# An attention-plus-MLP kernel on one core: the hand order of head pairs 0 to 17 written anew, banks taken by a ring, two halves of the norms issued apart, 67 zero products instead of 116

## The chip, the cores and the metric

The kernel runs on one core of a Trainium2 chip. A core has a matrix engine (PE, with its weight loads shown apart as PEld), a vector engine (DVE), a scalar engine (ACT), a general engine (POOL) and a queue engine (SP), each with its own instruction stream that is worked off in order, and DMA queues. The engines meet through semaphores. The metric is the device time of one execution in microseconds. A profiled execution gives the span and the trace; the times come from other executions, which carry no profile.

## The reference: what is computed

Cosine attention over 8 batches of 12 heads, 448 positions and 64 channels, then an MLP with a hard-swish between its two products:

```python
q_n = q / (np.linalg.norm(q, axis=-1, keepdims=True) + 1e-06)
k_n = k / (np.linalg.norm(k, axis=-1, keepdims=True) + 1e-06)
scores = np.matmul(q_n, k_n.transpose(0, 1, 3, 2)) / tau
...
attn = np.exp(scores)
attn = attn / (np.sum(attn, axis=-1, keepdims=True) + 1e-09)
return np.matmul(attn, v).astype(np.float32)
...
h = x @ w_in                          # x: 3584 x 768, w_in: 768 x 2048
relu6 = np.clip(h + 3.0, 0.0, 6.0)
g = h * relu6 / 6.0
return (g @ w_out).astype(np.float32) # w_out: 2048 x 768
```

Inputs and output are float32; tau is 0.1.

## The kernel before

The 96 heads are worked as 48 pairs, six pairs to a batch. The 448 positions of a head lie as 64 rows of 7 slots. An item `j` is the queries or the keys of two pairs, four heads (item 0 the queries and item 1 the keys of pairs 0 and 1, items 2 and 3 those of pairs 2 and 3, and so on; from item 14 on the order of queries and keys is turned round). An item is loaded, squared, reduced to its sums of squares, given its inverse norms, multiplied by them into bf16, and transposed. Items 0 to 13 are transposed on PE into a PSUM bank and copied out of it; from item 14 on a transposing DMA does it.

For each pair the scores come in four groups (three of two 128-key tiles, one for the last 64 keys of both heads), each is turned into exponentials by ACT, and PE multiplies the exponentials with the values and a column of ones, so that the row sums come along. DVE divides, and the result is transposed to be the input `xT` of the MLP of its batch: PE works six products for each 128 of the 2048 hidden channels (L591), ACT makes `u` (L608), DVE makes `gT` (L614). The second MLP product is taken as seven products over two by two blocks with sums of blocks formed beforehand on DVE (`w_sum` at L697, `gs` at L726, products at L751).

Nothing is scheduled by a planner at run time: the order on every engine is the order in which the Python code issues the instructions. For pairs 18 to 47 a loop issues them; for pairs 0 to 17, the start included, the order is written out by hand in `PLAN`, a list of strings whose words are operations. The words that the prediction uses, with the function and the line of each:

- `LQ.j`, `LV.d`: SP issues the load of an item (L201) and the four loads of the values of two pairs (L216). A buffer is loaded again only when its last reader is done.
- `SQ.j.e.c.n`: squares n of an item's slots from slot c on engine e (v for DVE, a for ACT, p for POOL; L231 or L233).
- `RE.j`: DVE adds the squares (L245).
- `NO.d`: the inverse norms of both items of d, first two small ACT instructions (L275, L276), then two on DVE where the word ends in v (L278, L279), two more on ACT where not. `NO.d.x` is one item. `NN.8` does two at once.
- `NM.j.e`: the item times its inverse norms (L292). With `.0` or `.1` behind it, one half.
- `TR.j`: seven transposes on PE into a bank (L338), which Y or Z behind it names. `XD.j`: the transposing DMA issued by SP (L349) with its two small POOL copies.
- `CQ.i`, `CK.i`, `CS.i`: queries and keys of pair i copied out of the bank or the transposed tile to where PE reads them (L358 ACT, L360 DVE, L388 DVE from the DMA's tile).
- `SC.i.g`, `EX.i.g`, `VA.i.g`, `FI.i`: scores (L441), exponentials (L459), values (L481) and the division (L501, L502).
- `BK.i`, `CX.i`: the transposes of the result on PE (L515) and the copy to `xT`; `XP`, `XB` do it by DMA.
- `VC.i`: the values of a pair cast to bf16 (L309, L311).
- `W`: POOL issues a load of weights (L921). `WS`, `GS`: sums of weight or activation blocks (L697, L726).
- `UH.n.k`, `U`: parts of the first MLP product, whole units of either product; `UA` and `UV` issue the ACT and DVE work that such a unit leaves (`u`, `gT`).
- `DP.n`: n zero products into a corner of the bank PV that nobody reads (L933). `D.1`: one into Y.

PSUM has eight banks. Two are PV. Until `OPEN` (after the exponentials of pair 5) four serve as two wide score buffers `SC0` and `SC1`; Y and Z are named by the words for transposes. From `OPEN` on, the four and Y and Z form a ring of six, out of which each result takes the next bank, while some words still name Y or Z:

```python
bank = {"Y": Y, "Z": Z}[name] if name else next_bank()
```

A bank is written again when its last reader is done; that wait stands on PE.

Of the kernel before, what the change touches and what calls it, by code (L numbers as in the profile page):

```python
# [66 lines left out]
def kernel(
# [857 lines left out]
    def busy(n):  # L925
        bank_of("Y", 0)
        for _ in range(n):
            nc.tensor.matmul(Y[:, :], zeros[:, 0:128], zeros[:, :], start=True, stop=True)
# [182 lines left out]
```

## Time and profile before

| what | before |
|---|---|
| median of 3 executions | 401.87 us (401.65 to 402.15) |
| the profiled execution's span | 403.6 us |
| PE busy, matmuls | 394.2 us, 98% |
| DVE busy | 297.2 us, 74% |
| ACT busy | 277.4 us, 69% |
| POOL busy | 233.1 us, 58% |
| zero products | 116 into PV, 18.3 us of PE's busy time |

The span of the profiled execution is 1.7 us above the median of those without a profile. Busy shares are means over the whole span; the front, where the items of the first pairs are prepared, differs from the rest, so the prediction reads the profile by stretches. In a timeline row the first number is the start in us, the second the time in which the row's instructions ran, then engine, line, operation, the tile written and read, the shapes and the count; brackets hold the idle time ahead of it and what ended it. Instructions of one engine overlap by some tenths of a microsecond, so a row's time is a little more than the distance to the next start.

### The profile page before, as it was taken

Reading aid. Unit: us, or ns where it says so; the run is one execution under the profiler, and the core shown is the slowest. Engines: PE = TensorE matmul, PEld = TensorE weight load, DVE = VectorE, ACT = ScalarE, POOL = GpSimd, SP = SyncE. Lnnn points to the kernel's source line nnn. Section 1 sums busy time; section 2 is a strip of 40 time slices with the busy share of each in tenths; the row PEclk is TensorE's granted clock in tenths of the full one; section 3 lists DMA queues with packets and bytes.
Section 4 is the critical chain, followed back from the end, with each engine's and each line's share of the span. In section 5 each row is a group of like instructions: output and inputs, shape, how many; then the busy total and the mean of one; then the engine's idle time right before and its main releaser. Section 6 shows DMA issues by size and latency. Waiting matters only on the chain.

```text
span 403.6 us, 9692 instructions
## 1 busy us (share of the span) xinstructions
PE 394.2 (98%) x3708; PEld 234.7 (58%) x3709; DVE 297.2 (74%) x535; ACT 277.4 (69%) x602; POOL 233.1 (58%) x234
## 2 busy tenths in 40 slices
PE   8999999989999999999999999999999999999996
PEld 7666556545565556555555556555565556555563
DVE  7898898899868777767867887587656566654663
ACT  5799889886677686786858768668758755225230
POOL 6799709660675896479385876866665500510070
PEclk9999999999999999999999999999999999999999
DMA  8989989998679469696899647866883523130134
GB/s 288 291 209 231 222 179 278 168 231 203 173 149 242 97 149 198 170 200 135 174 209 206 151 118 167 179 184 137 192 154 72 112 45 66 42 79 21 24 74 98
DMA packets 93166, 63.75 MB, mean 158 GB/s; under 512 B 56128, under 2 KB 93120, under 8 KB 93120
## 3 DMA queue, kind: packets, MB, share of 16 engines
q1 hardware_dynamic: 87408, 56.45, 60.9%
q0 software_dynamic: 5312, 6.29, 9.3%
q8 instruction: 29, 0.48, 0.5%
q10 hardware_dynamic: 400, 0.39, 0.3%
q14 instruction: 17, 0.14, 0.1%
HBM read 45.61 MB, written 11.01 MB: 140 GB/s over the span
## 4 chain that ended last, share of the span: by engine, by line
PE 80%; DVE 5%; POOL 4%; DMA 3%; issue 3%; ACT 3%; SPq 0%; POOLq 0%; DVEq 0%
PE M L591 21%; PE M L751 17%; PE PV L481 10%; PE Y L751 6%; PE M L441 5%; PE Z L751 5%; PE Z L591 4%; PE Y L591 3%; PE M L831 3%; ACT at L459 2%; DMA big<-in_k_dram 2%; POOL nrm L292 2%; POOL big L233 2%; DMA tT<-nrm 2%; PE Z L831 1%
## 5 line engine op out<-in xcount | busy, mean ns | idle before, releaser
L591 PE MATMUL M<-xT,w_in_sb 128*128 128x448 bf16 x540 | 114.6, 352 | 0.2 <-DVE gT L614 0.2
L459 ACT ACTIVATE at<-M 128x448 bf16<-128x448 f32 x195 | 96.7, 566 | 20.0 <-PE M L441 10.1
L591 PEld LDWEIGHTS <-w_in_sb 128*128 128x128 bf16 x768 | 72.3, 98 | 64.2 <-issue 3.8
L233 POOL TENSOR_TENSOR big<-big 128x896 f32<-128x896 f32 (+5 forms) x47 | 69.5, 1481 | 23.0 <-DMA big<-in_k_dram 10.4
L292 POOL TENSOR_TENSOR nrm<-big,r 128x896 bf16<-128x896 f32 (+1 forms) x45 | 74.6, 1660 | 10.2 <-ACT r L282 5.5
L614 DVE SCALAR_TENSOR_TENSOR gT<-u,M 128x448 bf16<-128x448 bf16 x80 | 48.9, 617 | 35.2 <-ACT u L608 34.7
L608 ACT ACTIVATE u<-M,bias 128x448 bf16<-128x448 f32 x90 | 58.1, 651 | 22.9 <-PE M L591 22.2
L481 PEld LDWEIGHTS <-at 128*128 128x128 bf16 (+1 forms) x1536 | 53.8, 97 | 20.4 <-issue 10.6
L481 PE MATMUL PV<-vx,at 128*128 128x65 bf16 (+1 forms) x1536 | 62.2, 193 | 0.1
L245 DVE TENSOR_REDUCE n<-big 128x14 f32<-128x896 f32 (+1 forms) x50 | 51.6, 1038 | 2.1 <-POOL big L233 1.9
L398 POOL COPY km<-tT 64x128 bf16<-64x128 bf16 x34 | 12.7, 373 | 59.1 <-PE M L441 25.1
L780 POOL TENSOR_TENSOR big<-big 128x384 f32<-128x384 f32 x12 | 12.4, 1036 | 59.4 <-ACT big L799 59.4
L751 PEld LDWEIGHTS <-gT 128*128 128x128 bf16 x320 | 30.8, 98 | 22.0 <-DVE gT L726 0.8
L502 DVE TENSOR_TENSOR on<-PV,rc 128x512 bf16<-128x512 f32 x48 | 33.2, 691 | 1.7
L441 PE MATMUL M<-tT,kz 64*128 64x448 bf16 (+1 forms) x175 | 31.7, 351 | 1.7 <-DVE gT L614 1.4
L751 PEld LDWEIGHTS <-gs 128*128 128x128 bf16 x248 | 23.7, 98 | 16.3 <-DVE gs L726 0.8
L459 ACT ACTIVATE at<-Y 128x448 bf16<-128x448 f32 x51 | 28.8, 565 | 6.1 <-PE Z L441 6.0
L751 PE MATMUL M<-w_out_sb,gT 128*128 128x384 bf16 x176 | 32.2, 326 | 0.3 <-DVE gT L726 0.3
L459 ACT ACTIVATE at<-Z 128x448 bf16<-128x448 f32 x48 | 27.0, 562 | 3.8 <-PE M L441 1.9
L751 PE MATMUL M<-w_sum,gs 128*128 128x384 bf16 (+1 forms) x168 | 29.1, 318 | 0.0
L726 DVE TENSOR_TENSOR gs<-gT 128x1024 bf16<-128x1024 bf16 x30 | 28.9, 962 | 0.0
L591 PE MATMUL Z<-xT,w_in_sb 128*128 128x448 bf16 x132 | 28.6, 352 | 0.0
(131 smaller groups left out, 569.7 us busy)
## 6 DMA issues: line engine op xcount, KB each, us to landing
big<-in_k_dram SPq DMA_DIRECT2D x24, 448.0 KB, 4.6
big<-in_q_dram SPq DMA_DIRECT2D x24, 448.0 KB, 4.7
out_dram<-o SPq DMA_DIRECT2D x107, 96.0 KB, 2.2
big<-in_v_dram SPq DMA_DIRECT2D x48, 128.0 KB, 4.2
big<-in_v_dram SPq DMA_DIRECT2D x48, 96.0 KB, 4.2
w_in_sb<-in_moe_w_in_dram POOLq DMA_DIRECT2D x8, 384.0 KB, 7.8
w_out_sb<-in_moe_w_out_dram POOLq DMA_DIRECT2D x4, 768.0 KB, 11.7
tT<-nrm SPq DMA_TRANSPOSE x34, 3.0
```

Of the source, the lines that this page charges most:

```text
L233: engines[e].tensor_tensor(out=o, in0=i, in1=i, op=ALU.mult)
L245: nc.vector.tensor_reduce(out=n2_and_r[0][:, d % 2, j % 2, c], in_=sq[:, :, :, :].rearrange("p g c d -> p (g c) d")[:, c, :], axis=AX.X, o ...
L292: engines[e].tensor_tensor(out=nrm[:, :, g, :].rearrange("p c g d -> p g c d"), in0=raw_of[j][:, g, :, :], in1=n2_and_r[2][:, d % 2, j % 2, :]
L441: nc.tensor.matmul(o, ks, qt[rows], start=True, stop=True)
L459: nc.scalar.activation(out=o, in_=x, func=AF.Exp, scale=inv_tau)
L481: nc.tensor.matmul(pv_out(j, h), at[rows, n, q_cols(i // HP, j)], vt[rows, 3 + h if name == "M" else 5 * h + int(name[1]), :], start=(name ...
L502: nc.vector.tensor_tensor(out=on[:, :, :, :].rearrange("p j h d -> p h j d"), in0=pv4[:, :, :, 0:D], in1=rc[:, :, :].to_broadcast([128, 2, ...
L591: nc.tensor.matmul(ps[:, 0:S], w_in_sb[:, cc, fc * 128 : (fc + 1) * 128], xT[b % 2][:, cc, 0:S], start=(cc == 0), stop=(cc == CC - 1), ski ...
L608: nc.scalar.activation(out=u[:, :], in_=ps[:, 0:S], func=AF.Relu, bias=half_bias, scale=1.0 / 6.0)
L614: nc.vector.scalar_tensor_tensor(out=g[:, fc, c0 : c0 + S], in0=u[:, :], scalar=1.0, in1=ps[:, 0:S], op0=ALU.min, op1=ALU.mult,)
L726: nc.vector.tensor_tensor(out=o[:, :, :], in0=x, in1=y, op=op)
L751: nc.tensor.matmul(m, lhs[:, c, :], rhs[:, c, c0 : c0 + width], start=(base is None and c == 0), stop=(c == KC - 1), skip_group_check=True,)
```

## The change

`PLAN` is replaced by another order of almost the same words. The words in which the two differ: 67 zero products (`DP`) instead of 116 and no `D.1`; `NO.d` split into `NA.d` (the two ACT instructions) and `NV.d` (the rest) for d of 0 to 7 and 10; `CK.3` on ACT instead of DVE, `CK.18` on DVE instead of ACT; `VC.12` on ACT instead of POOL, `VC.13` on POOL instead of ACT, `VC.18` on DVE instead of POOL, `VC.19` on ACT instead of DVE; `NM.20` on POOL instead of DVE. No transposes name their bank any more: each result's bank is given by one digit of `RING`, and behind its end the ring of six goes on.

```diff
 PLAN = [
-    "LQ.1 SQ.1.v.0.4 DP.3 DP.5 DP.1 DP.1 DP.1 DP.1 DP.2 DP.1 DP.2 DP.6 DP.2 DP.2 DP.1 DP.1 DP.2 DP.1 DP.1 DP.1",
-    "SQ.1.a.11.3 SQ.1.p.4.3 DP.1 DP.2 DP.3 SQ.1.a.7.4 RE.1.0 DP.1 DP.4 LQ.0 DP.2 SQ.0.p.0.6 DP.1 RE.1.1 DP.1 LQ.3",
-    "DP.1 SQ.3.p.0.4 DP.1 SQ.0.a.6.2 SQ.0.a.8.6 DP.1 DP.1 RE.0.0 DP.1 RE.0.1 LQ.2 NO.0.1 NM.1.v.0 NM.1.v.1 SQ.3.a.4.3",
-    "NO.0.0 NM.0.p.1 DP.2 DP.2 SQ.2.a.4.3 TR.1.Z NM.0.p.0 LQ.5 SQ.2.a.0.4 D.1 DP.1 RE.3 DP.1 CK.0.a SQ.5.p.0.4 DP.2",
-    "SQ.5.a.4.3 DP.2 RE.2 NO.1.v DP.3 DP.2 DP.1 TR.0.Y LQ.4 CQ.0.a SQ.4.p.4.3 DP.2 SQ.4.a.0.4 DP.3 NM.3.p DP.1 RE.5",
-    "CQ.1.v RE.4 LV.0 SC.0.0.0 LQ.6 DP.3 VC.0.v NM.2.v.1 EX.0.0 SC.0.1.1 NM.2.p.0 CK.1.v LQ.7 LQ.8 DP.5 EX.0.1",
-    "SC.0.2.0 EX.0.2 DP.1 VC.1.v DP.1 DP.1 SC.0.3.1 EX.0.3 DP.2 VA.0.0 DP.2 LV.1 SQ.6.p.0.7 VA.0.1 SC.1.0.0 NO.2.v",
-    "NM.4.v.1 SC.1.1.1 TR.2.Y DP.1 NM.4.p.0 SQ.7.a.4.3 DP.1 RE.6 DP.1 DP.1 EX.1.0 EX.1.1 SC.1.2.0 TR.3.Z EX.1.2",
-    "CK.2.v DP.1 CQ.2.v SQ.7.p.0.4 DP.1 DP.1 VA.0.2 VA.0.3 SQ.8.a.4.3 NM.5.p SC.1.3.1 VC.3.p LQ.10 FI.0 EX.1.3 LQ.9",
...
+    "LQ.1 SQ.1.p.4.3 LQ.0 SQ.1.a.11.3 SQ.0.p.0.6 SQ.1.a.7.4 SQ.1.v.0.4 RE.1.1 SQ.0.a.8.6 SQ.0.a.6.2 LQ.3 RE.1.0",
+    "NA.0.1 NV.0.1 SQ.3.a.4.3 SQ.3.p.0.4 LQ.2 RE.0.1 RE.0.0 NM.1.v.0 NA.0.0 NV.0.0 SQ.2.a.4.3 NM.0.p.0 NM.1.v.1 LQ.6",
+    "LQ.5 SQ.2.a.0.4 DP.6 DP.6 DP.6 DP.6 DP.6 DP.6 DP.6 DP.2 TR.1 CK.0.a RE.3 RE.2 NM.0.p.1 SQ.5.p.0.4 DP.6 DP.2 TR.0",
+    "CQ.1.v NA.1 SQ.5.a.4.3 NV.1.v CQ.0.a LQ.4 DP.6 DP.2 SC.0.0.0 SQ.4.p.4.3 CK.1.v SQ.4.a.0.4 RE.5 LV.0 NM.2.p.0",
+    "VC.0.v RE.4 NM.2.v.1 SC.0.1.1 EX.0.0 DP.5 SC.0.2.0 EX.0.1 LV.1 VA.0.0 SC.0.3.1 EX.0.2 DP.2 SC.1.0.0 NM.3.p",
+    "SQ.6.p.0.7 VC.1.v LQ.7 EX.0.3 LQ.8 SC.1.1.1 NA.2 EX.1.0 NV.2.v NM.4.v.1 VA.0.1 NM.4.p.0 TR.2 SQ.7.p.0.4 SC.1.2.0",
+    "SQ.7.a.4.3 EX.1.1 LQ.9 EX.1.2 VA.0.2 TR.3 RE.6 SC.1.3.1 LQ.10 VA.0.3 CK.2.v CQ.2.v SQ.8.a.4.3 FI.0 LQ.11",
+    "SC.2.0.0 EX.1.3 SC.2.1.1 NM.5.p LV.2 SQ.8.a.0.4 RE.7 RE.8 LV.3 EX.2.0 CK.3.a VA.1.0 VC.2.v VA.1.1 EX.2.1 VC.3.p",
...
```

The words around the stretch of 60 to 90 us, before and after:

```diff
-    "EX.11.3 UA TR.12 CQ.13.v SQ.16.p.6.1 UV CQ.12.a SQ.17.p.0.7 CS.13.v NO.7.v U VA.11.1 VA.11.2 NM.14.p UA UV LQ.19",
-    "SC.12.0 EX.12.0 VA.11.3.t FI.11 SC.12.1 RE.16 LQ.18 U LV.6 EX.12.1 VC.12.p UA LV.7 UV SC.12.2 BK.9 NM.15.p",
-    "SQ.18.p.4.3 U SQ.18.a.0.4 CX.9.v U RE.17 UA BK.8.Z VA.12.0 UV CX.8.v EX.12.2 UA BK.10 SC.12.3 EX.12.3 CX.10.v",
-    "VA.12.1 VC.14.p SQ.19.p.0.7 XD.15 BK.11 CX.11.a U UA UV RE.18 XD.14 SC.13.0 SC.13.1 EX.13.0 W W LQ.21 U VA.12.2",
-    "UV VA.12.3.t RE.19 SC.13.2 UA UV U EX.13.1 SC.13.3 VC.13.a UA NN.8 WS.1.0 NM.16.p WS.7.0 CK.15.v EX.13.2",
-    "SQ.21.p.4.3 CK.14.a U U NM.18.p WS.6.0 EX.13.3 CS.14.v FI.12 XD.16 U U UV SC.14.0 UA UA UV UV U VA.13.0",
...
+    "SQ.16.p.6.1 CQ.12.a U VA.11.1 UV NV.7.v UA VA.11.2 NM.14.p SC.12.0 EX.12.0 LV.7 VA.11.3.t LQ.18 SC.12.1 U UV",
+    "FI.11 EX.12.1 RE.16 VC.14.p UA SC.12.2 UV LV.6 VC.12.a BK.9 U CX.9.v SQ.18.p.4.3 U BK.8 SQ.18.a.0.4 NM.15.p",
+    "XD.14 UA UV VA.12.0 RE.17 EX.12.2 BK.10 CX.8.v SC.12.3 VA.12.1 UA XD.15 CX.10.v LQ.21 BK.11 EX.12.3 CX.11.a U",
+    "SC.13.0 UV SQ.19.p.0.7 UA RE.18 EX.13.0 U VA.12.2 UV RE.19 VA.12.3.t SC.13.1 SC.13.2 UA EX.13.1 UV U UA W NN.8 W",
+    "CK.14.a VC.13.p WS.7.0 EX.13.2 SC.13.3 NM.16.p CK.15.v EX.13.3 U U U SQ.21.p.4.3 WS.1.0 NM.18.p WS.6.0 U FI.12",
+    "UV UA UV SC.14.0 UA UV VA.13.0 U U SQ.21.a.0.4 CS.14.v RE.21 UA VA.13.1 LQ.23 UV GS.6 VA.13.2 EX.14.0 VC.15.a",
...
```

(From pair 14 on `CK` is a DVE copy whatever letter stands behind it.) The code beside it:

```diff
+RING = "233223223323450123450123450123450123450123450123450123450123450123450123450123450123450123501234501234501234501234501234501234501234501234501234"
...
-    ring = []
+    ring = [None, None, Y, Z, None, None]
     ring_n = [0]
 
     def next_bank():
+        n = ring_n[0]
         ring_n[0] += 1
-        return ring[(ring_n[0] - 1) % len(ring)]
+        return ring[int(RING[n]) if n < len(RING) else (n - len(RING) + int(RING[-1]) + 1) % len(ring)]
...
+    def norms_root(d, *items):
         needs(("NM", 2 * d - 4), ("NM", 2 * d - 3))
-        items = items or (0, 1)
+        items, tiles, pairs = norm_tiles(d, items)
         for x in items:
             needs(("RE", 2 * d + x))
...
+        root(tiles, pairs)
+
+    def norms_inverse(d, *args):
+        items, tiles, pairs = norm_tiles(d, args)
+        inverse(tiles, pairs, "v" in args)
         for x in items:
             issued.add(("NO", d, x))
...
+    def root(tiles, pairs):
         n2, le, r = tiles
         ln, nr = n2, pairs[:, :, :, 0]
         nc.scalar.activation(out=ln, in_=n2, func=AF.Ln)
         nc.scalar.activation(out=nr, in_=ln, func=AF.Exp, scale=0.5)
+
+    def inverse(tiles, pairs, on_vector):
...
-        bank = {"Y": Y, "Z": Z}[name] if name else next_bank()
+        bank = next_bank()
```

The loop for pairs 18 to 47, the MLP products and the loads' sizes are as before.

More of the change, by code (lines that the diff above doesn't have):

```diff
@@ L251, in reduce, with norm_tiles @@
         whole("RE", j, heads)
+    def norm_tiles(d, items):
+        items = tuple(x for x in items if x != "v") or (0, 1)
+        it = slice(items[0], items[-1] + 1)
+        return items, [t[:, d % 2, it, :] for t in n2_and_r], nr_eps[:, d % 2, it, :, :]
     def norms(d, *items):
-        on_vector, items = "v" in items, tuple(x for x in items if x != "v")
+        norms_root(d, *items)
+        norms_inverse(d, *items)
+    def norms_root(d, *items):
         needs(("NM", 2 * d - 4), ("NM", 2 * d - 3))
-        items = items or (0, 1)
+        items, tiles, pairs = norm_tiles(d, items)
         for x in items:
             needs(("RE", 2 * d + x))
-        it = slice(items[0], items[-1] + 1)
-        inverse([t[:, d % 2, it, :] for t in n2_and_r], nr_eps[:, d % 2, it, :, :], on_vector)
+        root(tiles, pairs)
+    def norms_inverse(d, *args):
+        items, tiles, pairs = norm_tiles(d, args)
+        inverse(tiles, pairs, "v" in args)
         for x in items:
@@ L268, in norms_two @@
         two = [t.rearrange("p e i c -> p (e i) c") for t in n2_and_r]
-        inverse(two, nr_eps.rearrange("p e i c x -> p (e i) c x"), on_vector)
+        pairs = nr_eps.rearrange("p e i c x -> p (e i) c x")
+        root(two, pairs)
+        inverse(two, pairs, on_vector)
         issued.update(("NO", x, y) for x in (d, d + 1) for y in range(2))
-    def inverse(tiles, pairs, on_vector):
+    def root(tiles, pairs):
         n2, le, r = tiles
@@ L276, in inverse @@
         nc.scalar.activation(out=nr, in_=ln, func=AF.Exp, scale=0.5)
+    def inverse(tiles, pairs, on_vector):
+        n2, le, r = tiles
+        nr = pairs[:, :, :, 0]
         if on_vector:
@@ L921, in next_weights @@
         nc.gpsimd.dma_start(out=o, in_=w)
[L925 to L928, printed above, removed]
     def busy_pv(n):
@@ L941, in open_ring @@
         m = [psum_m.tile([128, 512], FP32, name=f"M{n}", tag=f"M{n}") for n in range(4)]
-        ring.extend([m[0], m[1], Y, Z, m[2], m[3]])
+        ring[:] = [m[0], m[1], Y, Z, m[2], m[3]]
     def unit():
@@ L958 @@
     OPS = {
-        "LQ": load_qk, "LV": load_v, "W": next_weights, "SQ": square, "RE": reduce, "NO": norms, "NN": norms_two,
+        "LQ": load_qk, "LV": load_v, "W": next_weights, "SQ": square, "RE": reduce, "NO": norms, "NA": norms_root, "NV": norms_inverse, "NN": norms_two,
         "NM": normalise, "VC": vcast, "TR": transposes, "XD": crossbar, "XB": back_crossbar, "XP": back_two, "CQ": copy_q, "CK": copy_k, "CS": copy_k3, "SC": scores,
         "EX": exps, "VA": values, "FI": finish_values, "BK": back, "CX": copy_x, "U": unit, "UH": lambda n, k, bank=None: mm1_piece(0, n, CUTS[k], CUTS[k + 1], bank), "UA": lambda: finish_units("a"), "UV": lambda: finish_units("v"), "UP": lambda: finish_units("p"), "GS": lambda x, *n: g_sum(*((0, "e") if x == "e" else (-1, str(x)))),
-        "GL": g_left, "WS": lambda x, *h: weight_sums(str(x), *((h[0] * KC // 2, KC // 2) if h else (0, KC))), "UU": whole_units, "D": busy, "DP": busy_pv, "OPEN": open_ring,
+        "GL": g_left, "WS": lambda x, *h: weight_sums(str(x), *((h[0] * KC // 2, KC // 2) if h else (0, KC))), "UU": whole_units, "DP": busy_pv, "OPEN": open_ring,
     }
@@ L967, in do @@
         key = (op,) + tuple(a for a in args if isinstance(a, int))
-        if op not in ("RE", "NM", "LQ"):
+        if op not in ("RE", "NM", "LQ", "NA", "NV"):
             issued.add(key[:3] if op == "SC" else key)
```

51 rows, old and new, of the table PLAN are left out of this document.

## The prediction, made before the changed kernel had run

> **What bounds the kernel now.** I read the busy table by stretches first, then the zero products alone, then each engine's timeline where the tensor engine (PE) is not full. In the table by stretches the columns are the stretch and its length, then the busy time (and count) of PE, its weight loads, the vector engine (DVE), the scalar engine (ACT) and POOL, the granted clock, the DMA share and GB/s.
>
> ```profile
> span 403.6 us, 9692 instructions
> ```
>
> ```profile
> 0.00:10.00 10.00, 8.94 (x58) 7.13 (x59) 7.16 (x32) 5.82 (x16) 6.75 (x22) 1.00 0.82 289
> 10.00:17.00 7.00, 6.83 (x74) 4.81 (x72) 5.84 (x8) 5.73 (x13) 6.63 (x6) 1.00 1.09 304
> 17.00:24.00 7.00, 5.84 (x80) 3.97 (x81) 6.90 (x14) 6.01 (x10) 5.08 (x5) 1.00 0.83 228
> 24.00:36.00 12.00, 11.30 (x172) 7.38 (x168) 11.54 (x31) 11.81 (x22) 11.96 (x11) 1.00 1.01 242
> 36.00:45.00 9.00, 8.77 (x165) 6.14 (x164) 6.57 (x23) 7.93 (x18) 8.98 (x11) 1.00 1.13 208
> 45.00:80.00 35.00, 34.88 (x358) 19.87 (x357) 32.10 (x63) 31.78 (x69) 19.86 (x19) 1.00 1.07 206
> 80.00:90.00 10.00, 8.46 (x72) 4.41 (x70) 9.60 (x16) 8.24 (x18) 7.04 (x6) 1.00 1.16 228
> 90.00:404.00 314.00, 309.19 (x2744) 180.94 (x2742) 217.52 (x354) 200.06 (x441) 166.81 (x158) 1.00 0.62 137
> ```
>
> The same table for the zero products alone, which are PE's work only:
>
> ```profile
> 17.00:24.00 7.00, 1.99 (x13) 1.07 (x14) 1.00 0.83 228
> 24.00:36.00 12.00, 2.23 (x12) 0.88 (x12) 1.00 1.01 242
> ```
>
> From 45 us on PE is full but for 1.54 us in 80 to 90 (10.00 - 8.46) and the last stores. All its other loss lies in front: the first 10 us hold only zero products, and in 17 to 24 only 5.84 - 1.99 = 3.85 us of 7 are needed work. So the end moves by what the first 45 us and the stall at 80 gain or lose. In 24 to 36 ACT is busy 11.81 of 12, DVE 11.54, POOL 11.96: there the others set the pace, and PE's zero products (2.23 us) fill time that it would wait anyway.
>
> **The change, step by step.** *Fewer zero products before the first transposes.* 58 stand before TR.1 now, 44 after the change.
>
> ```profile
> 1.06 9.17 PE L933 MATMUL PV<-xT 128*128 128x248 bf16 x58 [1.06 <-DVE xT L978]
> 10.07 0.55 PE L338 MATMUL Z<-ident,nrm 128*128 128x128 bf16 x7
> 10.68 1.43 PE L933 MATMUL PV<-xT 128*128 128x248 bf16 x12
> 11.95 0.55 PE L338 MATMUL Y<-ident,nrm 128*128 128x128 bf16 x7
> ```
>
> Twelve of them take 11.95 - 10.68 = 1.27 us, 0.106 each. At that rate 58 would take 6.15 us; they took 10.07 - 1.06 = 9.01. If the surplus of 2.86 is products at twice the time, 27 of them ran at 0.212, until 1.06 + 27 x 0.212 = 6.8 us, although the clock column shows 1.00. Then 44 products end at 1.06 + 27 x 0.212 + 17 x 0.106 = 8.6 us. TR.1 needs NM.1, the two DVE multiplications below that end at 7.49 + 1.41 = 8.90. So TR.1 starts near 9.0, 1.07 earlier, and its copy CK.0 on ACT (10.66 below) comes forward about as much.
>
> ```profile
> 7.49 1.41 DVE L292 TENSOR_TENSOR nrm<-big,r 128x448 bf16<-128x448 f32 x2
> 8.83 2.07 DVE L245 TENSOR_REDUCE n<-big 128x14 f32<-128x896 f32 x2
> 12.02 0.21 DVE L278 TENSOR_REDUCE le<-nr 128x28 f32<-128x56 f32 x1 [1.12 <-ACT nr L276]
> 15.34 2.13 DVE L292 TENSOR_TENSOR nrm<-big,r 128x448 bf16<-128x448 f32 x1
> 17.39 0.38 DVE L360 COPY kz<-Z 128x448 bf16<-128x448 bf16 x1
> 17.69 0.67 DVE L309 TENSOR_REDUCE vx<-big 128x512 bf16<-128x512 f32 x1
> 18.88 0.62 DVE L292 TENSOR_TENSOR nrm<-big,r 128x448 bf16<-128x448 f32 x1
> ```
>
> ```profile
> 10.66 0.53 ACT L358 COPY kz<-Z 128x448 bf16<-128x448 bf16 x1 [1.01 <-PE Z L338]
> 11.51 0.22 ACT L275 ACTIVATE n<-n 128x28 f32<-128x28 f32 x1
> 13.52 3.01 ACT L459 ACTIVATE at<-SC 128x896 bf16<-128x896 f32 x4
> 18.23 2.54 ACT L459 ACTIVATE at<-SC 128x896 bf16<-128x896 f32 x3 [0.92 <-PE SC L441]
> 21.25 1.35 ACT L459 ACTIVATE at<-SC 128x448 bf16<-128x448 f32 x2
> 36.53 0.98 ACT L459 ACTIVATE at<-M 128x448 bf16<-128x448 f32 x2 [0.43 <-PE M L441]
> ```
>
> ```profile
> 8.79 1.84 POOL L292 TENSOR_TENSOR nrm<-big,r 128x448 bf16<-128x448 f32 x2 [0.90 <-ACT r L282]
> 10.59 1.82 POOL L233 TENSOR_TENSOR big<-big 128x512 f32<-128x512 f32 x2
> 12.77 2.58 POOL L292 TENSOR_TENSOR nrm<-big,r 128x896 bf16<-128x896 f32 x2 [0.35 <-DVE r L279]
> 15.31 1.68 POOL L233 TENSOR_TENSOR big<-big 128x896 f32<-128x896 f32 x1
> ```
>
> *The norms' halves.* RE.2 ends at 8.83 + 2.07 = 10.90. Today CK.0 and the square SQ.5 stand ahead of the ACT half, and DVE idles 1.12 us until 12.02. After, that half follows CK.0 at once: from 10.95, and DVE resumes 0.51 later (12.02 - 11.51), at 11.45; CQ.1 (a 0.38 us copy) fits into its idle time. On ACT come SQ.5 and CQ.0 (whose TR.0 waits for NM.0, 8.79 + 1.84 = 10.63) and SQ.4, about half a microsecond each: the first exponential at 12.85 instead of 13.52, the first four done at 15.9.
>
> *CK.1 ahead of RE.5, VC.0, RE.4 and NM.2.* Today CK.1 is last of these, at 17.39, and the next exponentials start at 18.23 after 0.92 us of idle ACT. After, CK.1 stands at 12.0; the exponentials of pair 1 wait for ACT itself and start near 16.2 (15.9 and the two small norm steps). That is 2.0 us, but ACT takes on work behind it: SQ.7's part, which stood before 18.23, and CK.3, which leaves DVE, each 0.53 at most and 0.4 where ACT's starts follow one another. So 1.2 at most reaches the ACT-bound stretch.
>
> *What feeds it.* The next query and key come through NM.2 on DVE. Its half takes 0.62 us at 18.88 but 2.13 at 15.34, beside POOL's square from 15.31 to 16.99: I read that as DVE waiting for POOL's instruction to end. After the change POOL goes 10.59, + 1.82 = 12.41, + 2.58 = 15.0 and starts the square there. DVE goes 12.0 (norms), CK.1 to 12.35, RE.5 to 13.35, VC.0, RE.4, and asks for NM.2 at 14.95 if V is there at 13.3, later otherwise. V's loads now stand behind one more 448 KB load (LQ.6 before LQ.5 and LQ.4):
>
> ```profile
> 3.81 2.73 SPq L216 DMA_DIRECT2D big<-in_v_dram  x4
> ```
>
> ```profile
> big<-in_v_dram SPq DMA_DIRECT2D x4, 128.0 KB, 7.0
> ```
>
> They are issued from 3.8 to 6.5 and land 7 us later, 11 to 13.5; one load more at the 289 GB/s of the first 10 us is 1.6 us: 12.4 to 15.1. I take the late case: NM.2 misses the gap at 15.0, waits for the square until 16.7 and ends at 17.2. Then VC.1 (0.67), the norms (0.5), NM.4 (0.62), RE.6 (1.03) and two copies (0.3 each where they follow one another) free SC.2 at 20.6, and its exponential 0.35 later, at 20.95. Today that one is the second of the two from 21.25, which end at 22.60; a wide one takes 2.54 / 3 = 0.85, so it starts at 21.75. Gain 0.8. A part of SQ.8 that follows it today comes before it, and CK.3 takes that place. In the early case it is the 1.2 of ACT's own sum. Two bounds, 0.8 and 1.2; I take 0.8. With V later still, even the 0.8 may go. From there to 36.53 ACT is full with the same work, so the gain is carried to the first MLP products and, PE being full, to 80 us.
>
> *The zero products taken out of the later stretches* cost nothing, as said; if PE became the bound there each removed one would even gain 0.106.
>
> *The stall at 80.*
>
> ```profile
> 77.40 0.62 DVE L614 SCALAR_TENSOR_TENSOR gT<-u,Y 128x448 bf16<-128x448 bf16 x1 [0.17 <-ACT u L608]
> 77.94 1.82 DVE L697 TENSOR_TENSOR w_sum<-w_out_sb 128x1536 bf16<-128x1536 bf16 x2
> 80.33 0.61 DVE L388 COPY kz<-tT 128x384 bf16<-128x384 bf16 x2 [0.57 <-DMA tT<-nrm]
> 80.86 2.15 DVE L697 TENSOR_TENSOR w_sum<-w_out_sb 128x1536 bf16<-128x1536 bf16 x1
> 83.77 1.14 DVE L614 SCALAR_TENSOR_TENSOR gT<-u,M 128x448 bf16<-128x448 bf16 x2
> ```
>
> ```profile
> 72.71 2.59 SPq L349 DMA_TRANSPOSE tT<-nrm  x2
> ```
>
> DVE waits in order for transposing loads, and the gT products that free PE's banks stand behind. SP issues XD.15 first today and XD.14 behind it; both go at 72.71 when NM.15 is done, and the second lands at 80.3. After, XD.14 is first and goes when NM.14 is done, some 3 us earlier, while NM.15 waits for one more square (0.8) and goes at about the same 72.7. DVE's order becomes CK.14, one weight sum, CK.15, two sums. From gT's end at 78.0 - 0.8 = 77.2: 0.3 + 0.91 + 0.3 + 0.91 + 2.15, then the 0.76 from 83.01 to 83.77 as today: 82.5, which is 1.2 before 83.77, so 0.4 more than the shift. Bounds: the stall vanishes (1.5) or grows (rival three).
>
> *Casts and norms moved between engines* (VC.12, VC.13, VC.18, VC.19, CK.18 and NM.20, 0.4 to 1.7 us each) land beyond 70 us, beside a PE that is full while the others have a fifth to a half of their time free; without that cover each would cost its own length. *Banks by name in one ring* adds no instruction: every result takes the next of six banks, so a transpose now waits for the reader of the sixth result before it. Bounds: nothing, or one wait like the stall at 80 (1.5). I take nothing, because that reader lies several microseconds back where PE is full.
>
> Sum: 0.8 + 0.4 = 1.2 us off the span, 403.6 to 402.4. The runs' median lies 1.7 below the span (401.87); I carry that over: 400.7.
>
> **The rivals.** *One: more is gained.* NM.2 meets the gap (1.2) and the stall at 80 goes (1.5): 2.7, 399.2. For it: DVE is ready 0.05 us before the gap closes if V is in time. Against: V's landing.
>
> *Two: nothing arrives at the end.* In 45 to 80 DVE and ACT are busy 32.10 and 31.78 of 35; another order there can make PE wait as much as it came early. Then 401.9. Against: the orders there differ in few places.
>
> *Three: slower, by the load in front of the weight sums.* The two sums at 77.94 now run while DVE waits for the loads; after, CK.14 stands ahead of all three. If its load lands no earlier than the pair today, at 80.33, the chain is 80.33 + 0.3 + 0.91 + 0.3 + 0.91 + 2.15 + 0.76 = 85.7, 1.9 behind today's 83.77: 403.8. It decides from a landing at 78.4 on. Against: its issue is 3 us earlier.
>
> *Four: PE falls to half clock in 13 to 24 us.* There it is little more than half busy without zero products. If half rate held, needed work of 3.85 us in 17 to 24 would take 7.7, 0.7 too much, and the 11.30 - 2.23 = 9.07 of the next 12 us would take 18.1 at worst; PE, full then, would warm again after some 6 us as at the start, so about 3 us are lost: 403.7. Against: the longest gap by my sums is under 2 us.
> [...]
>
> **How the numbers follow.** Forecast 0.50, rival one 0.18, two 0.15, three 0.09, four 0.08. About 0.2% (0.8 us) can be told from no change here. Faster: the forecast but for its edge (0.47) and rival one, 0.65; slower: rivals three and four, 0.16 with rounding; same 0.19. The likeliest case has 399.9 to 401.5 by its own bounds; the range takes in rival one with a little beyond it and reaches upward to 402.9, which leaves out most of three and four: 398.5 to 402.9.
>
> **What would show it.** After: first transposes near 9.0, first exponentials near 12.9, those of pair 1 near 16.2, no CK.1 at 17; DVE's NM.2 either about 0.6 us at 15 (rival one's first half) or stretched to 17.2; the first MLP product near 41.4 instead of 42.2; DVE's third weight sum ended before 81.8, and PE's gap after 80 us near 1.1. The prediction is wrong if ACT idles between 16 and 36, if zero products or matmuls double their time after 9 us, or if PE shows new waits between 45 and 80.

## The result, and the profile after

| | median | range |
|---|---|---|
| before, 6 executions beside it | 402.28 us | 401.65 to 405.45 |
| after, 6 executions | 407.17 us | 405.67 to 411.57 |
| after / before | 1.0109 | 95% interval 1.007 to 1.0147 |
| forecast | 400.7 us | 398.5 to 402.9 |

The change makes the kernel slower by 4.9 us. The profiled execution of after took 405.67 us; its span, with its busy table by stretches (columns as in the prediction):

```profile
span 403.8 us, 9601 instructions
```

```profile
0.00:10.00 10.00, 7.89 (x58) 6.29 (x59) 7.36 (x32) 6.22 (x17) 6.93 (x22) 1.00 0.82 291
17.00:24.00 7.00, 5.56 (x83) 3.72 (x83) 6.89 (x14) 6.95 (x14) 6.98 (x8) 1.00 0.92 274
45.00:80.00 35.00, 32.17 (x334) 18.60 (x333) 27.74 (x58) 28.18 (x61) 19.91 (x18) 0.95 1.03 215
80.00:90.00 10.00, 10.00 (x82) 5.24 (x81) 9.77 (x17) 9.09 (x21) 6.83 (x6) 1.00 0.96 203
```

In 45 to 80 us, where PE was full before (34.88 of 35), it now idles 2.83 us and the clock is at 0.95; the stall of before in 80 to 90 is gone. The front did what was forecast. PE, ACT and DVE by time:

```profile
1.06 6.83 PE L945 MATMUL PV<-xT 128*128 128x248 bf16 x44 [1.06 <-DVE xT L990]
8.94 0.56 PE L355 MATMUL Y<-ident,nrm 128*128 128x128 bf16 x7 [1.05 <-DVE nrm L309]
...
40.59 1.39 PE L608 MATMUL M<-xT,w_in_sb 128*128 128x448 bf16 x6
```

```profile
12.68 3.04 ACT L476 ACTIVATE at<-SC 128x896 bf16<-128x896 f32 x4
...
16.00 0.90 ACT L476 ACTIVATE at<-SC 128x896 bf16<-128x896 f32 x1
```

```profile
13.68 0.69 DVE L326 TENSOR_REDUCE vx<-big 128x512 bf16<-128x512 f32 x1 [0.34 <-DMA big<-in_v_dram]
...
15.28 0.62 DVE L309 TENSOR_TENSOR nrm<-big,r 128x448 bf16<-128x448 f32 x1
```

First transposes at 8.94 (forecast 9.0), first exponentials 12.68 (12.85), those of pair 1 at 16.00 (16.2); V landed in time and NM.2 took 0.62 us at 15.28, the early case. The first MLP product starts 1.64 us earlier than in the profile of before (40.59 against 42.23), which has:

```profile
42.23 0.55 PE L591 MATMUL M<-xT,w_in_sb 128*128 128x448 bf16 x2
```

All of it is lost again at 70. ACT and PE there, and the clock:

```profile
67.70 0.66 ACT L625 ACTIVATE u<-M,bias 128x448 bf16<-128x448 f32 x1
71.76 0.62 ACT L328 CAST vx<-big 128x512 bf16<-128x512 f32 x1 [3.40 <-DMA big<-in_v_dram]
72.28 0.62 ACT L232 ACTIVATE big<-big 128x512 f32<-128x512 f32 x1
72.81 0.61 ACT L625 ACTIVATE u<-Z,bias 128x448 bf16<-128x448 f32 x1
73.33 0.96 ACT L476 ACTIVATE at<-M 128x448 bf16<-128x448 f32 x2
```

```profile
72.43 0.40 PE L498 MATMUL PV<-vx,at 128*128 128x65 bf16 x8 [1.75 <-ACT vx L328]
73.91 0.58 PE L532 MATMUL M<-ident,on 128*128 128x128 bf16 x4 [1.08 <-ACT at L476]
...
75.54 1.96 PE L608 MATMUL Z<-xT,w_in_sb 128*128 128x448 bf16 x6
```

```profile
72.00:74.00 2.00, 0.49 (x10) 0.39 (x10) 0.54 (x2) 2.00 (x5) 0.00 (x0) 0.87 1.14 104
74.00:76.00 2.00, 2.00 (x19) 1.54 (x19) 2.00 (x5) 1.58 (x4) 0.84 (x1) 0.50 1.16 313
76.00:78.00 2.00, 2.00 (x10) 0.73 (x9) 1.20 (x2) 0.77 (x2) 2.00 (x3) 0.78 0.06 19
```

ACT's cast VC.12 waits 3.40 us for values, and the exponentials and `u` behind it wait with it. PE idles 1.75 us for the cast and 1.08 for the exponentials (2.83 together), then the clock falls to 0.50: six MLP products take 1.96 us where six at 69.16 took 1.30. The values are late for two reasons to be seen on SP and POOL of after:

```profile
56.35 2.96 SPq L217 DMA_DIRECT2D big<-in_v_dram  x4
59.36 0.59 SPq L202 DMA_DIRECT2D big<-in_k_dram  x1
60.00 3.58 SPq L217 DMA_DIRECT2D big<-in_v_dram  x4
```

```profile
59.49 1.58 POOL L938 DMA_DIRECT2D w_out_sb<-in_moe_w_out_dram  x2
```

In the plan of before LV.6 is ahead of LV.7; after, LV.7 goes first (56.35) and LV.6, which VC.12 needs first, is issued from 60.00 on, just behind two 768 KB loads of `w_out`. Before had its eight value loads in a row, LV.6 first, with a cast without a wait:

```profile
58.63 7.06 SPq L216 DMA_DIRECT2D big<-in_v_dram  x8
```

```profile
70.43 0.61 POOL L311 CAST vx<-big 128x512 bf16<-128x512 f32 x1
```

In all but five of the executions whose span is on record (2.2 to 2.9 us there) the time is the span and 1.7 to 2.1 us: 403.8 and 405.67 here, 399.2 and 401.06 below. So the execution that was profiled as before, span 403.6, stands for about 405.5 us (two others of before with that span took 405.53 and 405.58), 3.2 above the median of 402.28. It was a late one.

### The profile page after: what moved, and what is told of

The parts are those of the page before. It is cut to its first block, busy times and chain, and to the rows that moved or that the text cites. A ratio compares the mean times of both kernels' runs of the same rounds, so it can differ in the third digit from the quotient of the medians.

```text
span 403.8 us, 9601 instructions
## 1 busy us (share of the span) xinstructions
PE 390.5 (97%) x3659; PEld 231.9 (57%) x3659; DVE 292.7 (72%) x533; ACT 277.8 (69%) x604; POOL 234.7 (58%) x234
## 4 chain that ended last, share of the span: by engine, by line
PE 82%; ACT 7%; DMA 5%; DVE 3%; POOL 2%; issue 1%; SPq 0%; DVEq 0%; ACTq 0%
PE M L608 22%; PE M L768 17%; PE PV L498 10%; PE Z L768 6%; PE Y L608 5%; PE M L458 5%; PE Z L608 5%; ACT at L476 4%; PE Y L768 4%; DMA big<-in_q_dram 3%; PE M L848 3%; DMA big<-in_v_dram 2%; PE Y L848 2%; PE Z L458 1%; PE Y L458 1%; ACT big L232 1%
## 5 line engine op out<-in xcount | busy, mean ns | idle before, releaser
L476 ACT ACTIVATE at<-M 128x448 bf16<-128x448 f32 x201 | 99.5, 563 | 14.4 <-PE M L458 10.4
L608 PE MATMUL M<-xT,w_in_sb 128*128 128x448 bf16 x504 | 106.2, 352 | 0.0
L309 POOL TENSOR_TENSOR nrm<-big,r 128x896 bf16<-128x896 f32 (+1 forms) x46 | 76.3, 1662 | 11.4 <-ACT r L299 6.8
L631 DVE SCALAR_TENSOR_TENSOR gT<-u,M 128x448 bf16<-128x448 bf16 x73 | 44.8, 618 | 37.5 <-ACT u L625 37.2
L625 ACT ACTIVATE u<-M,bias 128x448 bf16<-128x448 f32 x84 | 54.8, 653 | 24.1 <-PE M L608 23.4
L768 PE MATMUL M<-w_out_sb,gT 128*128 128x384 bf16 x200 | 36.4, 326 | 0.0
L458 PE MATMUL M<-tT,kz 64*128 64x448 bf16 (+1 forms) x180 | 32.6, 352 | 0.0
L476 ACT ACTIVATE at<-Y 128x448 bf16<-128x448 f32 x46 | 25.9, 562 | 8.8 <-PE Z L458 8.8
L608 PE MATMUL Y<-xT,w_in_sb 128*128 128x448 bf16 x138 | 29.9, 353 | 0.0
```

Source lines behind the costliest of these rows:

```text
L309: engines[e].tensor_tensor(out=nrm[:, :, g, :].rearrange("p c g d -> p g c d"), in0=raw_of[j][:, g, :, :], in1=n2_and_r[2][:, d % 2, j % 2, :]
L458: nc.tensor.matmul(o, ks, qt[rows], start=True, stop=True)
L476: nc.scalar.activation(out=o, in_=x, func=AF.Exp, scale=inv_tau)
L608: nc.tensor.matmul(ps[:, 0:S], w_in_sb[:, cc, fc * 128 : (fc + 1) * 128], xT[b % 2][:, cc, 0:S], start=(cc == 0), stop=(cc == CC - 1), ski ...
L625: nc.scalar.activation(out=u[:, :], in_=ps[:, 0:S], func=AF.Relu, bias=half_bias, scale=1.0 / 6.0)
L631: nc.vector.scalar_tensor_tensor(out=g[:, fc, c0 : c0 + S], in0=u[:, :], scalar=1.0, in1=ps[:, 0:S], op0=ALU.min, op1=ALU.mult,)
```

## The experiments

My theory was the late load of LV.6; rivals were the cast's move to ACT by itself, the clock alone, and the place in SP's queue as against the shared DMA. "Before" is the kernel before run beside them: 402.69, 402.31 and 403.3 us in the three groups (a, c and d of the labels, b in the first). Since it moves by up to 1 us between groups, times of different groups are compared below only roughly; the ratios hold within each. Each kernel has 12 executions, c_wlate 6. Two more questions came up: what the front is worth, and why executions of before lie between 401 and 407.

| kernel | median | ratio to before, 95% interval | profiled span |
|---|---|---|---|
| a_v6first | 401.19 us | 0.9934 to 0.9989 | 399.2 us |
| a_cast12pool | 404.84 | 1.0026 to 1.0084 | 404.0 |
| a_fill12 | 404.69 | 1.0014 to 1.0071 | 402.3 |
| b_v7first | 403.65 | 1.0000 to 1.0053 | 401.8 |
| c_same | 405.43, one execution | none | 403.5 |
| c_dp58 | 401.84 | 0.9967 to 1.0018 | 400.4 |
| c_wlate | 409.26 | 1.0136 to 1.0202 | 407.6 |
| c_bdp44 | 403.00 | 0.9981 to 1.0046 | 398.8 |
| d_v6pool | 401.56 | 0.9939 to 0.9982 | 399.9 |
| d_ck1late | 402.18 | 0.9958 to 0.9999 | 400.3 |
| d_na1late | 401.91 | 0.9944 to 0.9996 | 400.4 |
| d_fill17 | 401.63 | 0.9941 to 0.9995 | 399.2 |

### a_v6first: the two value loads of after exchanged

```diff
-    "... SC.12.0 EX.12.0 LV.7 VA.11.3.t LQ.18 ...",
+    "... SC.12.0 EX.12.0 LV.6 VA.11.3.t LQ.18 ...",
-    "FI.11 EX.12.1 RE.16 VC.14.p UA SC.12.2 UV LV.6 VC.12.a BK.9 ...",
+    "FI.11 EX.12.1 RE.16 UA SC.12.2 UV LV.7 VC.12.a BK.9 ...",
-    "CK.14.a VC.13.p WS.7.0 ...",
+    "CK.14.a VC.13.p VC.14.p WS.7.0 ...",
```

(VC.14 casts what LV.7 loads, so it moves behind that load's new place.)

> Theory (a late load): in the changed kernel ACT's cast VC.12 waits 3.4 us for the values of pairs 12 and 13, whose loads were put behind those of pairs 14 and 15 and one more; PE idles 2.8 us there and then runs some 4 us at half clock. With the two value loads exchanged back that wait is under 0.5 us, PE idles under 0.4 us from 45 to 80 us, the mean clock is 0.999 again and the time falls to 398.5 to 400.5 us. Rival (too few zero products): the clock falls because fewer zero products keep PE warm, whatever the loads do; then time and clock stay near 405 to 407 us and 0.99 to 0.996.

Measured 401.19 us, 6.0 below after and 0.39% below before: one exchange undoes the whole loss. SP now issues LV.6 from 56.43 to 59.55, and POOL its two loads of `w_out` from 59.61, so the exchange puts LV.6 ahead of these too, as it is in before (58.63 against 62.80). The sign and the place are as the theory says; the time is 0.7 above what I expected, because I still reckoned from the late profile of before. PE in 68 to 80 (after had 9.17 of 12), and the cast on ACT, which no longer waits:

```profile
68.00:80.00 12.00, 12.00 (x104) 6.69 (x103) 11.25 (x20) 10.69 (x24) 8.82 (x9) 1.00 1.18 202
```

```profile
68.29 0.65 ACT L328 CAST vx<-big 128x512 bf16<-128x512 f32 x1
```

### a_cast12pool and d_v6pool: the cast VC.12 back on POOL, with the loads as changed and with the loads mended

```diff
-    "... UV LV.6 VC.12.a BK.9 ...",
+    "... UV LV.6 VC.12.p BK.9 ...",
```

(d_v6pool is the same edit on a_v6first, where the word before it is LV.7.)

> The changed kernel with the cast VC.12 on POOL again, the loads left in the changed order. If the late load itself is the cost (the values are needed by PE's VA.12.0), PE still idles 2 us or more near 71 us and the time stays at 404.5 to 407.5 us, with POOL waiting instead of ACT. If ACT's order is the cost (everything behind the cast on ACT waits with it), ACT's wait of 3.4 us goes, PE idles under 1 us there and the time is 400 to 402.5 us.

> a_v6first with the cast VC.12 back on POOL, as before the change. Theory (the cast moved to ACT costs nothing by itself, only the load behind it was late): within 0.6 us of a_v6first, 400.7 to 401.8, no wait of PE over 0.5 us in 68 to 78. Rival (ACT's cast is itself a loss, or POOL's a gain): 1 us or more below a_v6first.

404.84 and 401.56. With the loads as changed PE waits for the cast on POOL too; POOL and PE of a_cast12pool:

```profile
73.53 0.62 POOL L328 CAST vx<-big 128x512 bf16<-128x512 f32 x1 [3.57 <-DMA big<-in_v_dram]
```

```profile
74.19 0.40 PE L498 MATMUL PV<-vx,at 128*128 128x65 bf16 x8 [2.61 <-POOL vx L328]
```

With the loads mended the engine makes no difference that can be told (401.56 against 401.19). So the move itself costs nothing, as forecast. With late values the time is 407.17 with the cast on ACT, where the exponentials and `u` wait behind it, and 404.84 with it on POOL. The clock differs with it: the mean granted clock is 0.998 or more in eight of twelve executions of a_cast12pool and 0.996 or less in all six of after.

### a_fill12: after with 16 zero products ahead of VA.12.0

```diff
-    "XD.14 UA UV VA.12.0 ...",
+    "XD.14 UA UV DP.16 VA.12.0 ...",
```

> The changed kernel with 16 zero products (1.7 us at 0.106) on PE ahead of VA.12.0, where it idles. Theory with the clock as a share of its own: the products fill 1.7 of the 2.8 us of idle time, the clock stays at 0.998 or above, and the time is 1.5 to 3 us shorter: 403.5 to 405.5 us. If the clock costs nothing beyond the idle time: 406.5 to 407.5 us.

404.69. The wait stays, PE works through it, and the clock holds; PE at the place:

```profile
70.60 1.86 PE L945 MATMUL PV<-xT 128*128 128x248 bf16 x16
72.40 0.40 PE L498 MATMUL PV<-vx,at 128*128 128x65 bf16 x8
73.89 0.38 PE L532 MATMUL M<-ident,on 128*128 128x128 bf16 x4 [1.08 <-ACT at L476]
...
74.98 1.34 PE L608 MATMUL Z<-xT,w_in_sb 128*128 128x448 bf16 x6
```

The six products take 1.34 us again instead of 1.96. This splits the 6.0 us: 2.5 for the clock (407.17 - 404.69) and 3.5 for the wait itself (404.69 - 401.19). The 2.5 are not the price of the one fall at 74: between the profiled executions it is 1.5 us (403.8 - 402.3). The clock of 0.87, 0.50 and 0.78 in the three stretches from 72 to 78 us falls short of 1.00 by (0.13 + 0.50 + 0.22) x 2 = 1.70 us, which is 3.4 us at 0.50 and 0.0042 of 404 us; by this estimate the mean clock of 0.996 stands for about one such fall and the 0.992 and 0.987 of the other executions of after for two and three. Where the others lie was not profiled in after; four of the other kernels' profiles have one before 25 us.

### b_v7first: before with the loads exchanged and the cast on ACT

```diff
-    "SC.12.0 EX.12.0 VA.11.3.t FI.11 SC.12.1 RE.16 LQ.18 U LV.6 EX.12.1 VC.12.p UA LV.7 UV SC.12.2 ...",
+    "SC.12.0 EX.12.0 VA.11.3.t FI.11 SC.12.1 RE.16 LQ.18 U LV.7 EX.12.1 UA LV.6 UV VC.12.a SC.12.2 ...",
```

> The kernel before, its 116 zero products kept, with the two value loads exchanged and the cast VC.12 on ACT as in the changed kernel. Theory (a late load): ACT waits 2 to 4 us for it, PE idles, the clock falls below 0.998, and the time is 404.5 to 408 us. Rival (too few zero products): the time stays within 1 us of the kernel before, 401.3 to 403.3 us, at clock 0.999.

403.65, 1.0 above before, with a lower bound of the interval at no change: less than I expected. ACT's cast waited 2.27 us for the values in its profile and PE 0.69 and 0.86, and the clock held. Here too the loads of `w_out` (issued from 60.83) fall among those of LV.6. The same exchange costs less in this plan: a shorter wait (3.40 in after) and no fall.

### c_wlate: the two loads of w_out moved behind the values

```diff
-    "... SC.10.3 UA W UV W UA",
+    "... SC.10.3 UA UV UA",
-    "FI.11 EX.12.1 RE.16 VC.14.p UA SC.12.2 ...",
+    "FI.11 EX.12.1 RE.16 VC.14.p W W UA SC.12.2 ...",
```

> After with the two loads of w_out that stand before LV.6 moved behind VC.14.p, some 9 us later; the order of the value loads stays as changed. If LV.6 lands late because it shares the DMA engines with these two loads: its last piece lands within 6 us of its issue (8.8 in after), ACT's cast waits under 0.7 us (3.40), time 401.5 to 404. If it is late by its place in SP's queue alone: it lands 8 us after its issue or more, the cast waits 3 us, time 406 to 408. In both cases the second half of the weight sums may wait for w_out, up to 2 us of DVE.

409.26: the mechanism came as expected, the time did not. SP, ACT and the stretches:

```profile
59.90 3.48 SPq L217 DMA_DIRECT2D big<-in_v_dram  x4
```

```profile
68.14 0.65 ACT L328 CAST vx<-big 128x512 bf16<-128x512 f32 x1
```

```profile
60.00:70.00 10.00, 10.00 (x113) 5.99 (x109) 8.86 (x22) 9.91 (x23) 6.69 (x7) 1.00 0.54 126
80.00:90.00 10.00, 4.61 (x25) 2.03 (x24) 5.35 (x9) 0.83 (x3) 0.21 (x2) 0.83 1.17 214
```

LV.6 is issued where after has it (59.90 against 60.00), yet the cast does not wait at all, where after's waits 3.40 us: the DMA share in 60 to 70 is 0.54, where after has 1.08 and a_v6first 1.09 in the same stretch. So the values were late through sharing with `w_out`, not through SP's order alone; either of the two mended is enough. But PE then idles 5.39 us at 81 and the kernel is slower than after:

```profile
86.61 0.56 PE L458 MATMUL M<-tT,kz 64*128 64x448 bf16 x2 [5.39 <-DMA tT<-nrm]
```

Two things are late there: DVE's first weight sum waits 4.74 us for `w_out` and starts at 81.26, with the `gT` products behind it, and a transposing load lands 13.5 us after its issue, where after's longest takes 6.1. The profile puts PE's wait down to the load; what the late weight sums alone would have cost was not told apart. I had put the cost at 2 us at most, on DVE.

### c_same and c_bdp44: before once more, and with 44 zero products

```diff
-    "LQ.1 SQ.1.v.0.4 DP.3 DP.5 DP.1 DP.1 DP.1 DP.1 DP.2 DP.1 DP.2 DP.6 DP.2 DP.2 DP.1 DP.1 DP.2 DP.1 DP.1 DP.1",
+    "LQ.1 SQ.1.v.0.4 DP.3 DP.5 DP.1 DP.1 DP.1 DP.1 DP.2 DP.1 DP.1 DP.1 DP.1 DP.1 DP.1",
```

(c_bdp44; c_same changes nothing.)

> The kernel before, unchanged, for a second profile. Theory (the profiled execution of before was a late one, its zero products at half rate until 6.8 us and two waits more): a span of 399 to 401.5, the last of the 58 zero products at half rate before 5.5 us, first transposes at 8.9 to 9.1, first MLP product at 41.0 to 41.4, and less than 0.7 us of idle PE in 80 to 90 us. Rival (that profile was typical and the span just lies 1.7 above the time): span 403 to 404, first transposes at 10.0, first MLP product at 42.2, 1.5 us idle in 80 to 90.

> Before with 44 instead of 58 zero products ahead of the first transposes, all else unchanged. Theory: first transposes at 8.9 to 9.1 whatever the moment at which the clock rises, first MLP product at 41.0 to 41.4; median 401.5 to 402.7 (at most 0.8 below before, since only executions with a late rise gain), with a clock of 0.99 in at most one of twelve, as 12 zero products still follow the transposes and 19 the first scores. Rival (the zero products before TR.1 set the start in every execution of before): median 1 us or more below before.

c_same met a late execution again, 405.43, with the same two marks (late first transposes, the stall at 80), so my expectation of a typical one fell; in both profiles the marks go with a time some 3 us above the median. Its PE and its stretch:

```profile
1.06 8.87 PE L933 MATMUL PV<-xT 128*128 128x248 bf16 x58 [1.06 <-DVE xT L978]
9.77 0.55 PE L338 MATMUL Z<-ident,nrm 128*128 128x128 bf16 x7
```

```profile
80.00:90.00 10.00, 8.46 (x72) 4.41 (x70) 9.72 (x15) 8.24 (x18) 7.04 (x6) 1.00 1.16 227
```

Its front has something else besides: between 8 and 42 us ACT waits 2.7 us and POOL 3.0 us for loads of keys, where the profile of before has no wait for a load. So its late first MLP product, at 42.42, has two possible reasons.

c_bdp44 was caught in an early execution, span 398.8. Its PE, DVE and ACT, with the order of before:

```profile
8.91 0.56 PE L338 MATMUL Z<-ident,nrm 128*128 128x128 bf16 x7 [0.49 <-DVE nrm L292]
...
40.11 0.55 PE L591 MATMUL M<-xT,w_in_sb 128*128 128x448 bf16 x2
```

```profile
14.71 0.64 DVE L292 TENSOR_TENSOR nrm<-big,r 128x448 bf16<-128x448 f32 x1
15.27 0.38 DVE L360 COPY kz<-Z 128x448 bf16<-128x448 bf16 x1
...
78.09 0.95 DVE L697 TENSOR_TENSOR w_sum<-w_out_sb 128x1536 bf16<-128x1536 bf16 x1
```

```profile
12.37 3.01 ACT L459 ACTIVATE at<-SC 128x896 bf16<-128x896 f32 x4
...
16.11 2.54 ACT L459 ACTIVATE at<-SC 128x896 bf16<-128x896 f32 x3
```

In such an execution the old order already has NM.2 in 0.64 us, pair 1's exponentials at 16.11 and the first MLP product at 40.11, ahead of after's 40.59 (b_v7first, with all 58 zero products, also has its first transposes at 8.89 and NM.2 in 0.68 us); and the third weight sum takes 0.95 us, not 2.15, with no stall at 80. The reason lies on POOL, in before and in c_bdp44:

```profile
80.51 1.69 POOL L292 TENSOR_TENSOR nrm<-big,r 128x896 bf16<-128x896 f32 x1 [3.36 <-ACT r L282]
```

```profile
78.40 2.18 POOL L292 TENSOR_TENSOR nrm<-big,r 128x896 bf16<-128x896 f32 x1 [3.36 <-ACT r L282]
```

Before, the sum (80.86) started 0.35 us behind POOL's multiplication and took 1.2 us longer; in c_bdp44 it started 0.31 ahead, and POOL's took 0.5 longer. The two other profiles with this order agree: in c_same the sum started 0.07 behind and took 2.43 us, in b_v7first 0.32 ahead and took 0.95, with no stall at 80. The copies ahead of the sum had waited 0.57 us for transposed tiles; without that it would, by these times, have been first here too.
The median of c_bdp44, 403.00, is no better than before and above the 401.5 to 402.7 that I expected, and 5 of its 12 executions took 404 to 406, two of them at a clock of 0.996; a late rise can hardly explain them, since with the latest rise seen, at 6.8, 44 products end by 8.6. What makes those late stays open; late loads are one candidate. b_v7first shows ACT waiting 1.04 us for keys at 16.78 and the first MLP product at 41.16 with the rest of its front close to c_bdp44's; d_v6pool, with after's front, shows DVE waiting 1.08 us for values ahead of 14.77 and the first MLP product at 41.80, though its clock holds there.

### c_dp58 and d_fill17: more zero products in a_v6first

```diff
-    "LQ.5 SQ.2.a.0.4 DP.6 DP.6 ...",
+    "LQ.5 SQ.2.a.0.4 DP.14 DP.6 DP.6 ...",
```

(c_dp58. d_fill17 adds DP.4 behind VA.0.1, DP.4 behind VA.0.2 and DP.6 behind VA.0.3.)

> After with the order of the two value loads mended (as in a_v6first) and 14 more zero products ahead of the first transposes, 58 as before the change. Theory (fewer zero products at the start let the clock fall in some executions): no execution with a mean clock under 0.997, none more than 2.5 us above the fastest from that cause, median 400.9 to 402, first transposes 8.9 to 10.1 by when the clock rises. Rival (the falls have another cause): one or two of twelve executions at a clock of 0.99 and 3 us more, as in a_v6first.

> a_v6first with 14 more zero products spread over 16 to 22 us. Theory (the executions of a_v6first near 404 at a clock of 0.99 come from PE being half idle there): no execution of twelve under 0.997, median 400.9 to 401.8, since PE has 1.5 us to spare there. Rival (they come from the 1.4 us gap before the first transposes, or from elsewhere): one to three of twelve stay at 0.99 and 3 us more.

401.84 and 401.63: neither gains on 401.19. Executions with a mean clock below 0.997 were one of twelve in each, two in a_v6first, none of 93 of before. So zero products do not cure the falls for certain, against what I expected of both; c_dp58's own profile has one, from 21.4 to 24.8 us.

### d_ck1late and d_na1late: the front's two moves undone in a_v6first

```diff
-    "CQ.1.v NA.1 SQ.5.a.4.3 NV.1.v CQ.0.a LQ.4 DP.6 DP.2 SC.0.0.0 SQ.4.p.4.3 CK.1.v SQ.4.a.0.4 RE.5 ...",
-    "VC.0.v RE.4 NM.2.v.1 SC.0.1.1 ...",
+    "CQ.1.v NA.1 SQ.5.a.4.3 NV.1.v CQ.0.a LQ.4 DP.6 DP.2 SC.0.0.0 SQ.4.p.4.3 SQ.4.a.0.4 RE.5 ...",
+    "VC.0.v RE.4 NM.2.v.1 CK.1.v SC.0.1.1 ...",
```

(d_ck1late. d_na1late has "SQ.5.a.4.3 NA.1" for "NA.1 SQ.5.a.4.3".)

> a_v6first with CK.1 behind NM.2.v.1 again, where it stood before the change. Theory (that move is what the front gains): exponentials of pair 1 at 16.8 to 17.4 instead of 16.1, the first MLP product 0.5 to 0.9 later than its 40.65, the time 0.4 to 1.0 above a_v6first: 401.6 to 402.2. Rival (something else holds ACT's chain): first MLP product within 0.2 of 40.65.

> a_v6first with the square SQ.5 on ACT ahead of NA.1 again, as before the change. Theory (with the transposes at 9.0 the square fits into the 0.83 us in which ACT waits for RE.2, so splitting the norms is worth nothing): NA.1 still at 10.9 to 11.0, first exponentials 12.3 to 12.8, first MLP product at 40.3 to 40.7, time within 0.5 of a_v6first. Rival (the prediction's step): NA.1 0.4 to 0.5 later, the first exponentials at 13.1 or later, the time 0.4 or more above.

402.18 and 401.91, 1.0 and 0.7 above a_v6first, but the intervals of the three overlap, and six of twelve executions of each had a clock below 0.997. Both profiles caught such a fall, so they tell little of the moves: from the first transposes to the first MLP product it is 32.46 us with CK.1 late (9.05 to 41.51) and 32.51 with it early in a_cast12pool (8.97 to 41.48), which fell too. In d_na1late NA.1 came at 11.57, behind a square that waited 0.70 us for its load: in that execution the square did not fit into ACT's idle time, though I had expected it to. Whether either move is worth something when the clock holds is not settled. The fall itself, PE of d_ck1late and of a_v6first:

```profile
9.05 0.56 PE L355 MATMUL Y<-ident,nrm 128*128 128x128 bf16 x7 [1.75 <-DVE nrm L309]
...
11.43 1.86 PE L945 MATMUL PV<-xT 128*128 128x248 bf16 x8
```

```profile
8.99 0.56 PE L355 MATMUL Y<-ident,nrm 128*128 128x128 bf16 x7 [1.39 <-DVE nrm L309]
...
11.08 1.01 PE L945 MATMUL PV<-xT 128*128 128x248 bf16 x8
```

## Why the prediction was wrong, point by point

- **The step that failed: "Casts and norms moved between engines".** I costed the moved words by their engines' free time, put them at nothing, and did not look at what the cast reads. The engine indeed costs nothing (d_v6pool); but the same lines of the diff put LV.7 ahead of LV.6, which moved LV.6 from 58.63 to 60.00 while POOL's loads of `w_out` came forward from 62.80 to 59.49 and so ahead of it. The cover I named, "a PE that is full", was gone for 2.83 us. Cost against a_v6first: 6.0 us, 3.5 of waiting and 2.5 that go with the clock. Two of the signs of being wrong that I named came, new waits of PE between 45 and 80 and products at half rate after 9; ACT did stay busy from 16 to 36 (19.45 of 20 us). (`CK.18`, which I listed among the moved words, did not move: from pair 14 on `CK` is a DVE copy in both kernels.)
- **The base.** "The runs' median lies 1.7 below the span; I carry that over" was wrong: an execution takes some 1.9 above its own span, so the profile of before showed an execution 3.2 above the median. The steps on the front and the stall at 80 were gains on that late execution. Part of them the old order has already in other executions: b_v7first, with all of its zero products, has its first transposes at 8.89 and no stall at 80, and c_bdp44 is ahead of after at the first MLP product. So they could not be taken off the median. That a_v6first, which lacks only the late load, comes within 0.5 us of the forecast is therefore luck as far as these runs show.
- **Fewer zero products, norm halves, CK.1, NM.2:** the times came as forecast, NM.2 in its early case, so 1.64 us arrived at the first MLP product instead of 0.8, on the profile of before; against b_v7first (41.16) it is 0.57, against the early c_bdp44 -0.48. Zero products removed in the later stretches cost nothing that shows.
- **The stall at 80** was to shrink by 0.4; it is gone. I read the long weight sum as the sum's own length; it was POOL starting first.
- **Rival three** did not come: PE is full in 80 to 90. **Rival four**, half clock in 13 to 24 us, did not come in after's profile but in three others of its front (0.76 in 10 to 17). Of these a_cast12pool has no late load beside it: its first MLP product comes at 41.48, 0.9 us behind after's, not 3. A fall lasted 3.4 us by the clock column, not the 6 that I took from the start. "The longest gap by my sums is under 2 us" was no argument against this rival: that a gap so short is harmless was not shown, and in d_ck1late a gap of 1.75 us ahead of 9.05 was followed by a fall at 10.74. The fall that after's profile shows came at 73.5, behind a wait that no rival held.
- **The ring** cost nothing in sight: no new wait of PE between 45 and 70.

What the front leaves is steadiness rather than speed: a_v6first's fastest execution is close to that of before (400.66 and 401.00), but 10 of 12 stay below 402.2, which 13 of 35 of before do. Its median is 0.4% below before's; d_v6pool repeats that with the same ratio, 0.9961.

## What to carry to other kernels

When an operation changes engine or place, follow its operands back to the load that feeds them: what else is in that load's queue, and which large loads on other queues move in those microseconds (here the wait of 3.40 us was gone in c_wlate, with POOL's two loads of `w_out` moved away). Before costing a stall at its length in one profile, compare that execution's own time with the median; in a late execution a stall can be a race lost by 0.3 us that other executions win.
